# Rest tokens' loads behind the first pair's, four more operand slots at a change of blocks, and less on GpSimd, in a three-stage kernel on one core

## The chip, the cores and the metric

The kernel runs on one core of one Trainium2 chip. The metric is device time in microseconds (us) of one execution; lower is better. The times before come from three runs, and one further execution was recorded by the hardware profiler. TensorE (PE) does the matmuls, VectorE (DVE), ScalarE (ACT) and GpSimd (POOL) the element-wise work, and SyncE (SP) issues every data transfer.

## The reference

Three stages follow each other on 2304 tokens (4 batches of 576) of width 512.

```
q_s, k_s = q * scale, k * scale                       # 4 batches, 8 heads, seq 576, head_dim 64
phi(x): h = x @ omega.T - sum(x*x)/2;  exp(h - max(h)) / sqrt(128)
kv  = einsum('bhsm,bhsd->bhmd', phi(k_s), v);  z = sum of phi(k_s) over s
att = (phi(q_s) @ kv) / (phi(q_s) . z + 1e-6)
x   = att as 2304 x 512
y   = relu(x @ w_in)**2 @ w_out                       # first feed-forward, d_ff 2048
xn  = y / sqrt(mean(y*y) + 1e-6) * rms_g
out = (silu(xn @ w_gate) * (xn @ w_val)) @ w_out2     # second feed-forward, d_ff 1536
```

## The kernel before

**Tiles.** The tokens lie in five blocks: blocks 0 to 3 hold 512 tokens each (the first 512 of a batch), and the rest block holds the last 64 tokens of each batch, 256 in all. An fp32 operand is split into a high part (a cast on ACT, L403) and a low part (source minus high part, L394, on DVE or POOL); a product is then three fp32r matmul passes: high by high and the two mixed ones.

**Stages.** For each batch the attention goes over four pairs of heads; features of k and q are matmuls at L601, and k features times v at L671 (L674 for the rest tokens). A batch's rest tokens need three loads of their own, made by `rem_prep`: rest_t (the transposed tokens), rest_r (their rows, for the norms) and rest_v. The first feed-forward takes 16 chunks of 128 of its hidden width per block, at L845 (into PSUM bank h) and L875 (into acc), block by block between attention work; the rest block comes last, and L894 (DVE) and L890 (ACT) copy its results out of PSUM. Its output y goes to DRAM and is read back by the second feed-forward, which normalises it: `rms` finds the row factors, `scaled` loads a tile of y and multiplies it (L1020, DVE).

**The second feed-forward** runs on two groups of blocks: blocks 0 and 1, then blocks 2 and 3 with the rest block. In a group, a kind (gate or value) of a pair of chunks of 256 hidden columns by two blocks is made of seven products instead of eight (`seven`, L1081): they need sums and differences of the operands, called B11, T1, T2, T3, B22, B21 and T4. `operands` makes these per half (two halves kk of the width): four `scaled` loads, four subtractions (`minus`, L928), seven splits (`in_two`). The second half's loads wait for the last `minus` of the first (`gates`). The weights' sums are made beforehand and stored; `read_unit` loads them as tiles wq and splits them. `plus` (L1101, DVE) adds products up in tiles cc; `gated` makes silu (L1123, ACT) times value (L1126) and splits it into tiles ub (or g); `out_rows` multiplies those by the output weights (L1142) and adds into tiles oa (L1150, DVE).

**Order.** A planner (`Plan`) writes out the order of every engine's instructions ahead of time. Each piece of work has a priority (a due time), an engine or a choice of two ("ANY" in a split means DVE or POOL; `both_sbuf` and one branch of `gated` choose in the same way), and buffers that come from fixed numbers of slots by class: x 16, xa 12, xb 4, f 4, st 3, wq 8 and so on. Whatever the planner picked is what the engines execute, in order. `FILL` sets up to which planned time the planner puts matmuls of ones that compute nothing (L486, in pairs) where it sees TensorE without work. `lead` is the priority of the rest tokens' loads. SP issues all loads and stores in planned order.

Between the two groups, operands of the second group take slots: temporaries (`room`) from classes st and xb, the split operands from x and xa; xb also holds the loads of `rms`, and f its row factors.

Of the kernel before, what the change touches and what calls it, by code (L numbers as in the profile page):

```python
# [15 lines left out]
ALU = mybir.AluOpType  # L16
# [26 lines left out]
class Plan:  # L43
# [9 lines left out]


    COLD = 6.9
    FILL = (0.6, 65.0, 0.21)
    SPARE = {"DVE": 1.0, "ACT": 0.2, "POOL": 0.2}
    SPARE_TO = 200.0
    LAT = 0.27
# [45 lines left out]
    def fill(self):  # L105
        n = Node()
        n.eng, n.dur, n.tail, n.prio, n.idx = "PE", self.FILL[2], 0.0, 0.0, -1
        n.bufs, n.acq, n.outs, n.deps, n.alts = [], [], [], set(), []
# [139 lines left out]
def kernel(  # L248
# [23 lines left out]
    nc = tc.nc  # L272
# [35 lines left out]
    plan = Plan(slots)  # L308
# [60 lines left out]
    def f32(t):  # L369
        return t.bitcast(F32)  # L370
# [5 lines left out]
    def dve(n):  # L376
        return 0.07 + n * 0.00104

    def pool(n):
        return 0.19 + n * 0.00216  # L380
# [154 lines left out]
    def attention(b):  # L535
        base = (b - 1) * float(C1) if b else -25.0
        step = 3.7 if b else 6.0
        lead = base - (6.0 if b else 3.95)
        full, long = b < FULL, b >= LONG
        rem_x = []  # L540
        ssr = Buf(["sm"])
# [365 lines left out]
    NC2 = C2 // 2  # L907
# [4 lines left out]
    G0 = [E1, E1 + NC2 + 2.0]  # L912
# [10 lines left out]
            decode(pos, st, lambda: w.ap, w)  # L923
        return w

    def both_sbuf(prio, out, in0, in1, op, n, rd, wr):
        def tt(en):
            return lambda: en.tensor_tensor(out=out(), in0=in0(), in1=in1(), op=op)  # L928

        plan.add("DVE", Shared(dve(n)), prio, tt(nc.vector), rd, wr, alts=[("POOL", pool(n), tt(nc.gpsimd))])  # L930

    last = []

# [30 lines left out]
    def read_unit(c, nm, pos, gates):  # L964

        u = Buf(["wq"])
        dma(pos, lambda: f32(u.ap[:, 1, :]), lambda: w2_d[c, nm], 262144, r=[b_w2d[c, nm], b_w2a], w=[u], after=gates)
        split(pos, lambda: f32(u.ap[:, 1, :]), lambda: u.ap[:, 0, :], lambda: u.ap[:, 1, :], 512, [(u, 1)], (u, 0), (u, 1),
              "ANY")
        return u  # L970

    def read_units(c, pos, gates):
# [51 lines left out]
        return x  # L1024

    def minus(p0, out, a, b, n):
        both_sbuf(p0, lambda: out.ap[:, :n], lambda: a.ap[:, :n], lambda: b.ap[:, :n], ALU.subtract, n, [a, b], [out])

    def in_two(p0, x, cls, n):

        xh, xl = Buf(cls), Buf(cls)
        split(p0, lambda: x.ap[:, :n], lambda: xh.ap[:, :n], lambda: xl.ap[:, :n], n, [x], xh, xl, "ANY")
        return xh, xl

    def operands(j, rv, p0, cls, gates, room):
# [82 lines left out]
    def gated(prio, g, v, in_psum):  # L1118

        uh, ul = Buf(["ub", "g"]), Buf(["ub", "g"])  # L1120
        sb = Buf(["cc"]) if in_psum else g
        plan.add("ACT", act(512), prio,
                 lambda: nc.scalar.activation(out=sb.ap, in_=g.ap, func=AF.Silu), [g], [sb])  # L1123

        def mul(en):
            return lambda: en.tensor_tensor(out=sb.ap, in0=v.ap, in1=sb.ap, op=ALU.mult)  # L1126

        if in_psum:
            plan.add("DVE", dve(512), prio, mul(nc.vector), [v, sb], [sb])
        else:  # L1130
            plan.add("DVE", Shared(dve(512)), prio, mul(nc.vector), [v, sb], [sb], alts=[("POOL", pool(512), mul(nc.gpsimd))])
        split(prio, lambda: sb.ap, lambda: uh.ap, lambda: ul.ap, 512, [sb, b_w2b], uh, ul, "ANY")
        return uh, ul

# [97 lines left out]
    room = ["st", "dw"]  # L1232
# [4 lines left out]
    plan.add("NONE", 0.0, 0.0, open_w2b, w=[b_w2b], after=ph1_nodes)  # L1237
    sets = [read_units(c, E1 + (c - 1.0 if c else -7.0), []) for c in range(NC2)]
    hidden0 = moe2(0, sets, x01, None)
    room = ["st", "xb"]  # L1240
    rvr = rms(REM, G0[0] + 0.7, hidden0[:1], ["xb"], room, ["f"])
    xr2 = operands_rem(rvr, G0[0] + 2.0, hidden0[:1], room)
    rv23 = [rms(j, G0[0] + j - 0.3, hidden0[j - 1:j], ["xb"], room, ["f"]) for j in range(2, 4)]
    x23 = operands(2, rv23, G0[0] + NC2 - 0.5, ["x", "xa"], hidden0[3:4], room)
    sets = [read_units(c, G0[1] + c - 1.0, hidden0[4:5]) for c in range(NC2)]
    moe2(1, sets, x23, xr2)
    with tc.manual_schedule():
# [71 lines left out]
```

## Time and profile before

| what | value |
|---|---|
| runs (three) | 1003.1, 1006.02, 1006.41 us; median 1006.02 |
| profiled execution, its own time | 1006.28 us |
| its span (first to last instruction) | 1004.5 us |
| mean granted TensorE clock | 0.996 |
| PE busy | 989.2 us, 98% of the span |
| DVE, ACT, POOL busy | 712.2, 525.6, 122.3 us |
| DMA | 179.36 MB, mean 179 GB/s |

Busy time counts the time in which an engine had an instruction under way. The span is 1.8 us shorter than the execution's own time, and a change of the span is taken as a change of the time.

### The profile page before, as it was taken

The page shows a single profiled execution, that of the slowest core. Times are in us where ns is not written, and L with a number is a line of the kernel's source. Part 1 is how long each engine was busy: PE and PEld are TensorE (multiplying, and loading weights), DVE is VectorE, ACT ScalarE, POOL GpSimd, SP SyncE. Part 2 cuts the span into 40 slices and gives each one's busy share as a digit, 9 for nine tenths or more (in the row PEclk, how much of TensorE's full clock was granted, in tenths as well). Part 3 has the DMA queues.
Part 4 walks back from the last instruction along what each step waited for, and adds up shares of the span by engine and source line. Part 5 has one row for each costly group of instructions (what it writes and reads, how often), then busy time and mean ns, then how long its engine had stood idle before and what let it go on. Part 6 is the DMA issues. An engine that isn't in the chain of part 4 may idle for free.

```text
span 1004.5 us, 14617 instructions
## 1 busy us (share of the span) xinstructions
PE 989.2 (98%) x5140; PEld 838.4 (83%) x5140; DVE 712.2 (71%) x1374; ACT 525.6 (52%) x1097; POOL 122.3 (12%) x101
## 2 busy tenths in 40 slices
PE   8999999999999999999999999999998999999998
PEld 7888888888888888888789978888886888888887
DVE  5989998577658576655622879889797747576673
ACT  5878888545564555544534557654353444224220
POOL 0110132131110101100000302311043000000000
PEclk9999999999999999999999999999999999999999
DMA  7777888976667575678868435234243212212213
GB/s 244 255 243 251 280 263 307 303 256 228 242 216 260 188 247 185 226 255 286 281 216 267 146 106 162 80 116 137 75 123 108 83 53 63 74 31 79 71 32 104
DMA packets 74841, 179.36 MB, mean 179 GB/s; under 512 B 8848, under 2 KB 12048, under 8 KB 74768
## 3 DMA queue, kind: packets, MB, share of 16 engines
q1 hardware_dynamic: 74768, 178.43, 54.2%
q8 instruction: 40, 0.66, 0.3%
q14 instruction: 33, 0.27, 0.1%
HBM read 143.27 MB, written 35.13 MB: 178 GB/s over the span
## 4 chain that ended last, share of the span: by engine, by line
PE 88%; DVE 4%; DMA 4%; issue 1%; ACT 1%; POOL 1%; SPq 0%; ACTq 0%; POOLq 0%; DVEq 0%
PE acc L875 18%; PE h L845 18%; PE acc L1081 11%; PE t L1142 11%; PE h L1081 10%; PE t L1081 3%; PE t L731 3%; PE t L604 2%; PE t L601 2%; PE t L671 2%; DMA st<-y 2%; PE t L726 1%; PE h L1142 1%; DVE cc L1101 1%; DVE wq L394 1%
## 5 line engine op out<-in xcount | busy, mean ns | idle before, releaser
L875 PE MATMUL acc<-g,wr 128*128 128x512 f32 (+1 forms) x660 | 151.7, 374 | 0.7 <-DVE g L394 0.7
L845 PE MATMUL h<-x,wr 128*128 128x512 f32 x528 | 133.4, 396 | 0.0
L875 PEld LDWEIGHTS acc<-g,wr 128*128 128x128 f32 x660 | 113.6, 189 | 21.3 <-DVE g L394 1.5
L1142 PE MATMUL t<-wq,ub 128*128 128x512 f32 x462 | 114.5, 392 | 0.7 <-DVE oa L1150 0.7
L1081 PE MATMUL acc<-x,wq 128*128 128x512 f32 x321 | 111.5, 396 | 1.8 <-DVE f L894 1.8
L845 PEld LDWEIGHTS h<-x,wr 128*128 128x128 f32 x528 | 97.2, 188 | 19.2
L403 ACT CAST wq<-wq 128x512 fp32r<-128x512 f32 x108 | 66.3, 619 | 87.3 <-DMA wq<-w2d4g 14.8
L1142 PEld LDWEIGHTS t<-wq,ub 128*128 128x128 f32 x462 | 86.7, 189 | 20.6 <-DVE oa L1150 2.4
L394 DVE TENSOR_TENSOR g<-f,g 128x512 fp32r<-128x512 f32 (+1 forms) x67 | 46.4, 693 | 70.1 <-ACT f L515 58.8
L859 ACT ACTIVATE f<-h 128x512 f32<-128x512 f32 (+1 forms) x80 | 44.9, 562 | 92.4 <-PE h L845 86.1
L1081 PE MATMUL acc<-xa,wq 128*128 128x512 f32 x231 | 89.9, 396 | 3.1 <-ACT xa L403 3.1
L394 DVE TENSOR_TENSOR wq<-wq 128x512 fp32r<-128x512 f32 x99 | 74.1, 756 | 25.5 <-ACT wq L403 25.0
L1081 PE MATMUL h<-x,wq 128*128 128x512 f32 x255 | 81.0, 390 | 0.0
L1081 PEld LDWEIGHTS acc<-x,wq 128*128 128x128 f32 x321 | 61.1, 191 | 15.1 <-DVE f L894 2.3
L875 PE MATMUL acc<-g,wu 128*128 128x512 f32 (+1 forms) x300 | 70.7, 376 | 0.2 <-DVE g L394 0.2
L1081 PE MATMUL h<-xa,wq 128*128 128x512 f32 x201 | 69.3, 390 | 0.4 <-DVE xa L394 0.4
L628 ACT ACTIVATE p<-t,sm 128x128 f32<-128x128 f32 x216 | 60.0, 383 | 18.1 <-DVE sm L619 18.1
L1101 DVE TENSOR_TENSOR cc<-acc,cc 128x512 f32<-128x512 f32 x84 | 57.7, 686 | 14.8 <-PE acc L1081 13.8
L1150 DVE TENSOR_TENSOR oa<-t,oa 128x512 f32<-128x512 f32 x75 | 50.8, 686 | 23.1 <-PE t L1142 22.7
L845 PE MATMUL h<-x,wu 128*128 128x512 f32 x240 | 61.6, 398 | 0.0
L875 PEld LDWEIGHTS acc<-g,wu 128*128 128x128 f32 x300 | 51.5, 189 | 9.5 <-DVE g L394 0.8
L441 ACT ACTIVATE dw<-st 128x512 f32<-128x512 f32 x68 | 46.6, 696 | 22.8 <-DMA st<-in_w_out_dram 9.4
(245 smaller groups left out, 1818.8 us busy)
## 6 DMA issues: line engine op xcount, KB each, us to landing
wr<-w1d SPq DMA_DIRECT2D x88, 512.0 KB, 4.3
st<-in_w_out_dram SPq DMA_DIRECT2D x28, 512.0 KB, 4.7
w1d<-wr SPq DMA_DIRECT2D x22, 512.0 KB, 4.1
st<-in_w_in_dram SPq DMA_DIRECT2D x16, 512.0 KB, 4.5
st<-in_w_gate_dram SPq DMA_DIRECT2D x12, 512.0 KB, 5.9
st<-in_w_val_dram SPq DMA_DIRECT2D x12, 512.0 KB, 5.9
st<-y SPq DMA_DIRECT2D x23, 256.0 KB, 4.1
v<-in_v_r_dram SPq DMA_DIRECT2D x16, 260.0 KB, 3.2
```

What stands on the lines that cost most here:

```text
L394: return lambda: en.tensor_tensor(out=lo(), in0=src(), in1=f32(hi()), op=ALU.subtract)
L403: first = plan.add("ACT", act(n), prio, lambda: nc.scalar.copy(out=hi(), in_=src()), rd, [whi], after, pre=[blo] if blo is not bhi else [])
L441: lambda: nc.scalar.activation(out=out(), in_=hf(), func=AF.Abs, scale=65536.0), [(st, 1)], [w])
L628: nc.scalar.activation(out=pbuf.ap[:, j0 + i, :], in_=fp.ap[:, i, :], func=AF.Exp, bias=mx.ap[:, i:i + 1])
L731: nc.tensor.matmul(np.ap[:, r * D1:(r + 1) * D1], lhsT=qt.ap[:, r * P:(r + 1) * P], rhs=kvt[:, h, :], start=True, stop=True)
L845: nc.tensor.matmul(hb.ap[:, :n], lhsT=u.ap[:, wl, kk * P:(kk + 1) * P], rhs=xcols(j, xl, kk)(), start=(gi == 0 and ii == 0), stop=(gi == l ...
L859: lambda: nc.scalar.activation(out=rb.ap[:, :n], in_=hb.ap[:, :n], func=AF.Relu), [hb], [rb])
L875: nc.tensor.matmul(accs[e].ap[:, :n], lhsT=u.ap[:, w, es], rhs=x.ap[:, :n], start=(c == 0 and i == 0), stop=(c == C1 - 1 and i == 2))
L1081: nc.tensor.matmul(bank.ap[:, cols], lhsT=u.ap[:, wl, c0 + kk * P:c0 + (kk + 1) * P], rhs=x[kk][xl].ap[:, :cols.stop - cols.start], start= ...
L1101: lambda: nc.vector.tensor_tensor(out=out.ap, in0=bank.ap, in1=x.ap, op=ALU.add), [bank, x], [out])
L1142: nc.tensor.matmul(o.ap, lhsT=x[xl].ap[:, c0:c0 + P], rhs=us[f"o{i}"].ap[:, wl, :], start=i == n == 0, stop=i == 1 and n == 2)
L1150: lambda: nc.vector.tensor_tensor(out=oa.ap, in0=o.ap, in1=oa.ap, op=ALU.add), [o, oa], [oa])
```

## The change

```
--- before.py
+++ after.py
@@ -53,7 +53,7 @@
 
 
     COLD = 6.9
-    FILL = (0.6, 65.0, 0.21)
+    FILL = (0.6, 45.0, 0.21)
     SPARE = {"DVE": 1.0, "ACT": 0.2, "POOL": 0.2}
     SPARE_TO = 200.0
     LAT = 0.27
@@ -535,7 +535,7 @@
     def attention(b):
         base = (b - 1) * float(C1) if b else -25.0
         step = 3.7 if b else 6.0
-        lead = base - (6.0 if b else 3.95)
+        lead = base - (6.0 if b else 2.85)
         full, long = b < FULL, b >= LONG
         rem_x = []
         ssr = Buf(["sm"])
@@ -923,11 +923,12 @@
             decode(pos, st, lambda: w.ap, w)
         return w
 
-    def both_sbuf(prio, out, in0, in1, op, n, rd, wr):
+    def both_sbuf(prio, out, in0, in1, op, n, rd, wr, pool_too=True):
         def tt(en):
             return lambda: en.tensor_tensor(out=out(), in0=in0(), in1=in1(), op=op)
 
-        plan.add("DVE", Shared(dve(n)), prio, tt(nc.vector), rd, wr, alts=[("POOL", pool(n), tt(nc.gpsimd))])
+        plan.add("DVE", Shared(dve(n)), prio, tt(nc.vector), rd, wr,
+                 alts=[("POOL", pool(n), tt(nc.gpsimd))] if pool_too else [])
 
     last = []
 
@@ -966,7 +967,7 @@
         u = Buf(["wq"])
         dma(pos, lambda: f32(u.ap[:, 1, :]), lambda: w2_d[c, nm], 262144, r=[b_w2d[c, nm], b_w2a], w=[u], after=gates)
         split(pos, lambda: f32(u.ap[:, 1, :]), lambda: u.ap[:, 0, :], lambda: u.ap[:, 1, :], 512, [(u, 1)], (u, 0), (u, 1),
-              "ANY")
+              "DVE")
         return u
 
     def read_units(c, pos, gates):
@@ -1024,12 +1025,12 @@
         return x
 
     def minus(p0, out, a, b, n):
-        both_sbuf(p0, lambda: out.ap[:, :n], lambda: a.ap[:, :n], lambda: b.ap[:, :n], ALU.subtract, n, [a, b], [out])
+        both_sbuf(p0, lambda: out.ap[:, :n], lambda: a.ap[:, :n], lambda: b.ap[:, :n], ALU.subtract, n, [a, b], [out], False)
 
     def in_two(p0, x, cls, n):
 
         xh, xl = Buf(cls), Buf(cls)
-        split(p0, lambda: x.ap[:, :n], lambda: xh.ap[:, :n], lambda: xl.ap[:, :n], n, [x], xh, xl, "ANY")
+        split(p0, lambda: x.ap[:, :n], lambda: xh.ap[:, :n], lambda: xl.ap[:, :n], n, [x], xh, xl, "DVE")
         return xh, xl
 
     def operands(j, rv, p0, cls, gates, room):
@@ -1128,7 +1129,7 @@
         if in_psum:
             plan.add("DVE", dve(512), prio, mul(nc.vector), [v, sb], [sb])
         else:
-            plan.add("DVE", Shared(dve(512)), prio, mul(nc.vector), [v, sb], [sb], alts=[("POOL", pool(512), mul(nc.gpsimd))])
+            plan.add("DVE", Shared(dve(512)), prio, mul(nc.vector), [v, sb], [sb])
         split(prio, lambda: sb.ap, lambda: uh.ap, lambda: ul.ap, 512, [sb, b_w2b], uh, ul, "ANY")
         return uh, ul
 
@@ -1237,11 +1238,11 @@
     plan.add("NONE", 0.0, 0.0, open_w2b, w=[b_w2b], after=ph1_nodes)
     sets = [read_units(c, E1 + (c - 1.0 if c else -7.0), []) for c in range(NC2)]
     hidden0 = moe2(0, sets, x01, None)
-    room = ["st", "xb"]
+    room = ["st", "f"]
     rvr = rms(REM, G0[0] + 0.7, hidden0[:1], ["xb"], room, ["f"])
     xr2 = operands_rem(rvr, G0[0] + 2.0, hidden0[:1], room)
     rv23 = [rms(j, G0[0] + j - 0.3, hidden0[j - 1:j], ["xb"], room, ["f"]) for j in range(2, 4)]
-    x23 = operands(2, rv23, G0[0] + NC2 - 0.5, ["x", "xa"], hidden0[3:4], room)
+    x23 = operands(2, rv23, G0[0] + NC2 - 0.5, ["x", "xa", "xb"], hidden0[3:4], room)
     sets = [read_units(c, G0[1] + c - 1.0, hidden0[4:5]) for c in range(NC2)]
     moe2(1, sets, x23, xr2)
     with tc.manual_schedule():
```

The whole of it, in words. Fillers are planned up to 45 us of planned time instead of 65. The rest loads of batch 0 get a later priority. In the second feed-forward, the low part of the split weights and of the operands, the subtractions of `minus` and the product in `gated` can now go to DVE only; the split behind that product may still go to POOL. For the second group, temporaries come from st and f instead of st and xb, and the split operands may also take the four xb slots. From L931 on line numbers are one higher (L1082 is L1081 of before, L1151 is L1150, and so on).

By count, over the whole program: POOL has 18 fewer instructions of L394, one fewer of L928 and of L1126, and five more of L514 (squares for the attention's row norms). DVE has 18 more of L394, one more of L928 and L1126 each, two more of L437 and three fewer at L516 and L510. ACT has four fewer of L515, two fewer of L435 and two more of L509. PE has ten fewer matmul records of L486. SP has as many transfers as before.

**SP at the start of the program.** Names ahead of `<-` are buffers with their numbers; `in_k_t_dram` and so on are inputs. Before:

```order
L388 DMA om_76<-in_omega_t_dram 64x128 x2
L388 DMA lt_190<-in_rest_t_dram 128x512
L388 DMA ld_195<-in_rest_r_dram 128x512
L388 DMA vr<-in_rest_v_dram 64x520
L388 DMA lt_206<-in_k_t_dram 128x512
L388 DMA tt_215<-in_q_t_dram 128x512
L388 DMA ld_221<-in_k_r_dram 128x512
L388 DMA ld_229<-in_q_r_dram 128x512
L388 DMA v_82<-in_v_r_dram 128x520
```

With the change:

```order
L388 DMA om_76<-in_omega_t_dram 64x128 x2
L388 DMA lt_190<-in_k_t_dram 128x512
L388 DMA lt_195<-in_q_t_dram 128x512
L388 DMA ld_202<-in_k_r_dram 128x512
L388 DMA ld_211<-in_q_r_dram 128x512
L388 DMA v_82<-in_v_r_dram 128x520
L388 DMA tr_222<-in_rest_t_dram 128x512
L388 DMA ld_228<-in_rest_r_dram 128x512
L388 DMA vr<-in_rest_v_dram 64x520
```

The first pair's five loads (k and q in two layouts, v) moved ahead of the three rest loads; the eight together hold the same places as before.

**DVE where the first feed-forward ends and the second begins.** Buffers dw and st hold loaded and subtracted operands, x and xa their low parts, g low parts of the first feed-forward's rest block. Before:

```order
L928 TENSOR_TENSOR dw_6175<-dw_5607,dw_6175 128x512
L394 TENSOR_TENSOR x_6260<-st_5630,x_6259 128x512
L394 TENSOR_TENSOR x_6289<-dw_6175,x_6288 128x512
L928 TENSOR_TENSOR dw_6175<-st_5630,dw_6175 128x512
L516 TENSOR_TENSOR f_6306<-f_6306 128x256
L394 TENSOR_TENSOR g_6317<-f_6306,g_6316 128x256
L394 TENSOR_TENSOR x_6327<-dw_6175,x_6326 128x512
L1020 SCALAR_TENSOR_TENSOR st_6324<-wq_5279,g_sb,st_6324 128x512
L1020 SCALAR_TENSOR_TENSOR st_6334<-wq_5426,g_sb,st_6334 128x512
```

With the change:

```order
L928 TENSOR_TENSOR dw_6164<-dw_5597,dw_6164 128x512
L394 TENSOR_TENSOR x_6209<-st_5550,x_6208 128x512
L394 TENSOR_TENSOR x_6231<-dw_6164,x_6230 128x512
L1021 SCALAR_TENSOR_TENSOR st_5620<-wq_5269,g_sb,st_5620 128x512
L394 TENSOR_TENSOR g_6245<-f_6238,g_6244 128x256
L928 TENSOR_TENSOR dw_6164<-st_5620,dw_6164 128x512
L394 TENSOR_TENSOR x_6268<-st_5620,x_6267 128x512
L394 TENSOR_TENSOR x_6283<-dw_6164,x_6282 128x512
L394 TENSOR_TENSOR g_6289<-f_6274,g_6288 128x256
L1021 SCALAR_TENSOR_TENSOR st_6280<-wq_5269,g_sb,st_6280 128x512
L1021 SCALAR_TENSOR_TENSOR st_6295<-wq_5416,g_sb,st_6295 128x512
```

The last `minus` of the first half, on which the second half's loads wait, is `dw_6175<-st_5630` before and `dw_6164<-st_5620` with the change. It stood behind the low parts x_6260 (of B21) and x_6289 (of the difference T2); now B21's low part (x_6268) stands behind it, T2's (x_6231) is three rows ahead, and a g of the first feed-forward stands right ahead. The low parts of x that POOL made before are among DVE's rows now.

**ACT at the same place**: L859 takes the relu of the first feed-forward's h out of PSUM, so it waits for TensorE; L403 casts the second feed-forward's operands. Before:

```order
L403 CAST x_6259<-st_5630 128x512
L859 ACTIVATE f_6282<-h_6244 128x256
L403 CAST x_6288<-dw_6175 128x512
L861 ACTIVATE g_6295<-f_6282 128x256
L515 ACTIVATE f_6282<-f_6282 128x256
```

With the change:

```order
L403 CAST x_6230<-dw_6164 128x512
L859 ACTIVATE f_6238<-h_6191 128x256
L861 ACTIVATE g_6244<-f_6238 128x256
L515 ACTIVATE f_6238<-f_6238 128x256
L403 CAST x_6267<-st_5620 128x512
```

T2's cast (x_6288, now x_6230) stood behind an L859 and now stands ahead of the one that follows.

**PE where the second group of blocks takes over.** t and h at L1142 are results of `out_rows` of the first group; L1081 with x, xa or xb are products of the second group. Before:

```order
L1081 MATMUL acc_7992<-x_7735,wq_7945 128x512
L1081 MATMUL acc_7992<-x_7960,wq_7945 128x512
L1081 MATMUL acc_7993<-x_7795,wq_7949 128x512
L1081 MATMUL acc_7993<-xa_8012,wq_7949 128x512
L1081 MATMUL acc_7993<-x_7796,wq_7949 128x512
L1081 MATMUL acc_7993<-xa_8013,wq_7949 128x512
L1081 MATMUL acc_7993<-x_7795,wq_7949 128x512
L1081 MATMUL acc_7993<-xa_8012,wq_7949 128x512
L1142 MATMUL t_8030<-wq_7718,ub_7906 128x512 x2
L1142 MATMUL t_8030<-wq_7718,ub_7907 128x512
L1142 MATMUL t_8030<-wq_7756,ub_7867 128x512 x2
L1142 MATMUL t_8030<-wq_7756,ub_7868 128x512
```

With the change:

```order
L1143 MATMUL h_8018<-wq_7717,ub_7880 128x512 x2
L1143 MATMUL h_8018<-wq_7717,ub_7881 128x512
L1143 MATMUL h_8018<-wq_7755,ub_7852 128x512 x2
L1143 MATMUL h_8018<-wq_7755,ub_7853 128x512
L1143 MATMUL t_8029<-wq_7717,ub_7880 128x512 x2
L1143 MATMUL t_8029<-wq_7717,ub_7881 128x512
L1143 MATMUL t_8029<-wq_7755,ub_7852 128x512 x2
L1143 MATMUL t_8029<-wq_7755,ub_7853 128x512
L1082 MATMUL h_8041<-xb_7451,wq_7796 128x512
L1082 MATMUL h_8041<-x_7911,wq_7796 128x512
L1082 MATMUL h_8041<-xb_7452,wq_7796 128x512
L1082 MATMUL h_8041<-x_7912,wq_7796 128x512
```

Before, two products of the second group (12 rows, of which seven are shown) stood ahead of the last four row products of the first group; now all row products of the first group stand ahead of the second group's first product, whose operands are xb and x.

**DVE in the middle of the first group** has rows that make two of the second group's operands early, in slots of class xb. With the change:

```order
L1021 SCALAR_TENSOR_TENSOR st_7373<-f_6783,g_sb,st_7373 128x512
L1021 SCALAR_TENSOR_TENSOR st_7383<-f_7115,g_sb,st_7383 128x512
L1102 TENSOR_TENSOR cc_7440<-acc_7418,cc_7439 128x512
L928 TENSOR_TENSOR f_7456<-st_7383,st_7373 128x512
L394 TENSOR_TENSOR wq_7426<-wq_7426 128x512
L394 TENSOR_TENSOR wq_7430<-wq_7430 128x512
L394 TENSOR_TENSOR xb_7452<-st_7373,xb_7451 128x512
L1102 TENSOR_TENSOR cc_7441<-acc_7418,cc_7439 128x512
```

Before, no xb slot was open to these operands. Here the two L1021 rows, the `minus` into `f_7456` and the low part `xb_7452` belong to the second group; the rows of wq and cc among them belong to the first.

## Rows read from the trace of the kernel before

**Rows 1.** Profile page: the chain that ended last, share of the span by engine.
```profile
PE 88%; DVE 4%; DMA 4%; issue 1%; ACT 1%; POOL 1%; SPq 0%; ACTq 0%; POOLq 0%; DVEq 0%
```

**Rows 2.** Waits of PE: line, releaser; us in total, times, longest.
```profile
PE acc L1081 <- ACT xa L403: 3.1, 1, 3.1
PE acc L1081 <- DVE f L894: 1.8, 1, 1.8
...
PE h L1081 <- DVE xa L394: 0.4, 1, 0.4
```

**Rows 3.** Windows: length, PE, PEld, DVE, ACT, POOL busy (instructions), PE clock, DMA, GB/s.
```profile
584.00:588.00 4.00, 4.00 (x13) 3.12 (x12) 1.46 (x4) 2.63 (x4) 0.00 (x0) 0.57 0.23 70
762.00:766.00 4.00, 4.00 (x12) 2.69 (x12) 4.00 (x7) 1.24 (x2) 1.28 (x1) 0.63 0.17 66
```

**Rows 4.** Timeline from the start: begin, duration, engine, line; what ended the wait.
```profile
5.05 2.04 PE L601 MATMUL t<-bd,lt 128*128 128x256 f32 x4 [1.07 <-DMA lt<-in_rest_t_dram]
...
5.67 0.43 SPq L388 DMA_DIRECT2D v<-in_v_r_dram  x1
...
8.77 2.07 PE L601 MATMUL h<-bd,lt 128*128 128x256 f32 x4 [1.25 <-DMA lt<-in_k_t_dram]
...
17.08 1.00 PE L671 MATMUL h<-v,p 128*128 128x65 f32 x8
```

**Rows 5.** Windows of longer stretches, columns as in Rows 3.
```profile
25.00:125.00 100.00, 100.00 (x576) 85.28 (x576) 93.35 (x243) 83.34 (x202) 13.27 (x10) 1.00 0.77 259
600.00:765.00 165.00, 161.88 (x705) 132.69 (x704) 144.86 (x208) 87.57 (x152) 38.14 (x28) 0.99 0.37 109
743.00:765.00 22.00, 18.88 (x75) 14.55 (x74) 20.38 (x26) 7.72 (x14) 12.99 (x9) 0.92 0.20 66
```

**Rows 6.** Timeline, the last fillers.
```profile
58.77 1.78 PE L486 MATMUL acc<-ones 128*128 128x256 f32 x12
58.93 0.68 DVE L394 TENSOR_TENSOR x<-acc,x 128x512 fp32r<-128x512 f32 x1
```

**Rows 7.** Timeline, where the second feed-forward begins.
```profile
557.84 0.97 POOL L394 TENSOR_TENSOR g<-f,g 128x256 fp32r<-128x256 f32 x1 [2.81 <-ACT f L515]
...
567.32 0.38 ACT L859 ACTIVATE f<-h 128x256 f32<-128x256 f32 x1 [1.42 <-PE h L845]
...
568.97 0.69 DVE L928 TENSOR_TENSOR dw<-st,dw 128x512 f32<-128x512 f32 x1
...
572.24 1.41 DVE L1020 SCALAR_TENSOR_TENSOR st<-wq,g_sb,st 128x512 f32<-128x512 f32 x2
...
574.33 0.60 ACT L403 CAST x<-st 128x512 fp32r<-128x512 f32 x1
...
574.51 0.43 DVE L394 TENSOR_TENSOR g<-f,g 128x256 fp32r<-128x256 f32 x1 [0.87 <-issue]
...
574.99 1.57 PE L875 MATMUL acc<-g,wr 128*128 128x256 f32 x11 [0.39 <-DVE g L394]
...
582.80 0.75 DVE L894 COPY f<-acc 128x256 f32<-128x256 f32 x2
583.27 2.75 PE L1081 MATMUL acc<-x,wq 128*128 128x512 f32 x7 [1.84 <-DVE f L894]
```

**Rows 8.** Timeline, where the second group begins.
```profile
756.18 1.78 DVE L928 TENSOR_TENSOR st<-st,st 128x512 f32<-128x512 f32 x1
757.37 1.72 POOL L394 TENSOR_TENSOR x<-xb,x 128x512 fp32r<-128x512 f32 x1
...
761.56 0.79 PE L1081 MATMUL acc<-xa,wq 128*128 128x512 f32 x1 [3.12 <-ACT xa L403]
```

**Rows 9.** Groups by shape, 590 to 765: busy us, mean ns; idle before and releaser.
```profile
L1150 DVE TENSOR_TENSOR oa<-t,oa 128x512 f32<-128x512 f32 x26 | 17.5, 683 | 3.4 <-PE t L1142 3.4
L1126 DVE TENSOR_TENSOR cc<-cc,cc 128x512 f32<-128x512 f32 x17 | 13.5, 816 | 0.1
L394 DVE TENSOR_TENSOR ub<-cc,ub 128x512 fp32r<-128x512 f32 x15 | 12.6, 839 | 1.4 <-ACT ub L403 1.3
```

## Prediction: what the change should do to the time

> **What bounds the kernel now.** I read four views, in this order. The chain that ended last is 88% TensorE's [rows 1], and PE is busy for nearly the whole span, so a change pays only where PE idles or runs at a low clock. The waits of PE say where it idles: most of it is at two changes of stage, 3.1 us for operands of the second group and 1.8 us for a PSUM copy where the second feed-forward begins, with 0.4 us more at the latter [rows 2]. The windows add what the waits don't show: behind each of these idle stretches the granted clock falls. It is 0.57 over 584 to 588 and 0.63 over 762 to 766, which at full PE busy loses 4 x 0.43 = 1.7 us and 4 x 0.37 = 1.5 us [rows 3]. Third comes the start: PE waits 1.07 and 1.25 us for first loads, and the first real sum, k features times v, stands at 17.08 [rows 4]. Between these places PE is fully busy and no engine can win anything there.
>
> **The change, part by part.** The sum is made against the profiled execution, 1006.28 us, 0.26 above the median of the three runs, which is less than I can tell.
>
> *Rest loads behind the first pair's.* The load at the head of SP's queue is there at 5.05; the k load, which stood fourth, is there at 8.77 [rows 4]. So k's features can begin up to 8.77 - 5.05 = 3.7 us earlier. The product with v, however, also needs k's rows, v and, on PE and ACT, a turn among the rest tokens' work. The eight loads together hold the same places, so the last of them, issued at 5.67, does not come sooner. And what follows is not waiting for PE alone: from 25 to 125 DVE is busy 93% and ACT 83% [rows 5], so part of a head start is eaten there. Bounds 0 and 3.7; I take 1.2, a third.
>
> *No fillers behind 45 us of planned time.* Ten matmul records of PE go, in essence the twelve at 58.77. They hold PE until about 60.4 (58.77 + 1.6), whereas the low part that the next product awaits is ready at 58.93 + 0.68 = 59.61 [rows 6]. So 0.8 of the 1.6 us is gained, and the other 0.8 becomes a wait for DVE. Bounds 0 and 0.8, unless the clock falls (below). Together: 2.0.
>
> *Where the second feed-forward begins.* The last `minus` of the first half starts at 568.97, and only then are the second half's four loads issued, whose first L1020 follows at 572.24 [rows 7]. What made that `minus` late: ACT's cast of T2 stood behind an L859 that waited 1.42 us for TensorE [rows 7], and in the changed order that cast stands ahead of the L859. Also, DVE instructions beside POOL are stretched: an L928 that overlaps a POOL L394 takes 1.78 where DVE's undisturbed tiles of that size take 0.68, so 1.1 more [rows 8, 9], and the POOL splits of x are gone here. That is 1.42 + 1.1 = 2.5 us, more than the 1.84 that PE waits behind L894 [rows 7], whose DVE work is the tail of the same chain. So the 1.84 and the 0.42 go, and the clock's 1.7 in part, as it fell behind these. Against it: the last g low part, behind which PE waits 0.39, goes to POOL (0.97 for such a tile against DVE's 0.43, so +0.54), and a cast of 0.60 now stands ahead of its input on ACT [rows 7]. That wait becomes 0.39 + 0.54 + 0.60 = 1.5, and with it some of the clock's loss stays, 0.7 by my choice (less than half, as the idle stretch is shorter than the 2.65 of before). Gain: 0.39 + 0.42 + 1.84 + 1.7 - 1.5 - 0.7 = 2.1. Bounds: -1.1 (only the new 1.1 us of wait arrives) and 4.3 (all of it goes).
>
> *Where the second group begins.* Before, PE met the second group's products while DVE and ACT were still making operands, 3.12 idle at 761.56 [rows 8] and 1.5 at the low clock. Now two things come together. B11 and T2 of the first half are made early, into xb slots that were closed to them. And the first group's last four row products stand ahead: 161.88 us busy for 705 records is 0.23 each, 1.38 for the six of a product [rows 5], so 4 x 1.38 = 5.5 us more cover. Not all is covered: behind the last sum of the first group DVE has 34 instructions up to the first weight's low part. Each takes 0.68 [rows 9], about 0.62 from start to start, 21 us; PE's cover is 15 row products, 20.7 us. The waits for a PSUM bank and for ACT in that chain are worth some more, so I leave 1.0 us of idle or slow clock: 4.6 - 1.0 = 3.6. Bounds: 1.0 (DVE's chain as late as before, less the earlier two operands) and 4.6.
>
> *Off GpSimd.* Of POOL's 28 instructions from 600 to 765 [rows 5], 24 go to DVE: 19 of 512 columns at 0.683 and five of 256 at about 0.42, 15.1 us. DVE is idle there 165 - 144.86 = 20.1 us, so they fit, and the sharing gives some back: L1126 17 x (816 - 683) ns = 2.3 and the ub splits 15 x (839 - 683) ns = 2.3, 4.6 us in these two groups alone [rows 9]. Cost on PE: none while DVE runs ahead of it. In the last 22 us DVE idles only 1.6 [rows 5], but there POOL's nine become some 5.5 us of DVE against 13 us of overlap; this is in the 34 instructions above.
>
> The Trainium skill ("SBUF — State Buffer", section "SBUF: two separate sides") says that VectorE and GpSimd take one port pair as an exclusive lock, the other blocking for the whole instruction. The 1.78 against 0.68 agrees. By that rule alone the 24 instructions would give back as much DVE time as they took on POOL, by an estimate some 33 us (38.14 less the four that stay), and DVE would end up far lighter. The rows show only 4.6 in the two groups where it is plainest. By either DVE stays off the path of 600 to 743, so the sum is the same.
>
> **Sum:** 1006.28 - 2.0 - 2.1 - 3.6 = 998.6.
>
> **Rivals.**
>
> *The start's head start is hidden.* The first products need the rest tokens' loads or DVE and ACT anyway; then 1.2 of the first 2.0 goes, and a shortfall of 0.7 in the same crowded stretch is likely: 1000.5. For it: DVE's 93%. Against: PE plainly waits for k.
>
> *The clock falls where fillers were.* PE idles 0.8 us at 58.77 and runs below full clock after it, as it did behind both other idle stretches [rows 3]: the 0.8 gained becomes a loss of about 0.8, and if the wait of 1.5 keeps the whole 1.7 at 584 the term there is 1.1. 1006.28 - 0.4 - 1.1 - 3.6 = 1001.2. Against it: only longer idle shows a fall in these rows. The Trainium skill ("TensorE: Matmul & The Clock Gate", section "🔬 Part 1: The HAM clock gate (the "warmup" mystery)") speaks against the edit: the throttled state is the default there, and activity releases it. By that the twelve fillers had a use.
>
> *DVE's chains are not earlier.* What came off POOL fills the room that the changes of stage had: the terms there shrink to 0 and 1.0 and the start's to 1.2, 1004.1, hardly to be told from before. For it: DVE is full in the last 22 us. Against: the stretched rows become short.
>
> *DVE becomes the bound* in the first group, so slower: it takes 15.1 us more with nothing given back, in bursts that PSUM banks and cc tiles can't bridge. It decides from about 7.5 us (half) that PE sees, with the last term lost: 1006.28 - 2.0 - 2.1 + 7.5 = 1009.7. For it: ready casts wait behind what is queued on DVE. Against: 20 us of idle, and shorter rows.
>
> **How the numbers follow.** My forecast gets 0.52, and its own range is 996 to 1001; the hidden start 0.15, the clock 0.12, the late chains 0.13, slower 0.08. The time is the likeliest, 998.6. All terms at their best give 1006.28 - 3.7 - 0.8 - 4.3 - 4.6 = 992.9, which needs all at once, so the range begins at 994. It ends at 1004, in the case of the late chains, and leaves out that case's upper half, the slower one and the tails. A measurement of this kernel can't tell less than 0.3%, 3 us, from no change: below 1003.0 counts as faster, which holds the first three cases but for a tail, 0.78. The same: 0.14, mostly the late chains. Above 1009.0: 0.08.
>
> **What would show it.** Right: L671 begins near 15 to 16; no wait behind L894; the wait for g at the end of the first feed-forward 1 to 2 us; the wait at the second group's first product under 1 us and the clock of 0.63 gone; POOL's busy time some 33 us lower over 600 to 765 with DVE at over 150 of 165 and PE still busy. Wrong: L671 still at 17; a clock below 1.00 around 60; DVE without idle in 600 to 743 while PE shows waits on L1102, L1127 or ub; a new wait on xb or f, as the row factors and the temporaries now share four f slots.

## The result, and the profile after

The changed kernel takes 996.78 us (median of four runs, 995.74 to 997.85) against 1006.21 us of before (four runs, 1003.1 to 1007.34): ratio 0.9914, 95% interval 0.9893 to 0.9935. The forecast was 998.6 in a range of 994 to 1004. The profiled execution has a span of 994.4 us, 10.1 less.

First the waits of PE, columns as in [rows 2]:

```profile
PE t L601 <- ACT p L628: 1.9, 2, 1.7
PE t L1143 <- DVE oa L1151: 1.4, 5, 0.7
PE acc L875 <- DVE g L394: 1.4, 3, 1.0
PE t L601 <- DMA lt<-in_k_t_dram: 1.2, 1, 1.2
PE acc L875 <- POOL g L394: 1.2, 1, 1.2
```

The three rows of [rows 2] are gone, and what is left is small pieces. Three that matter below are new: 1.7 us for `p`, where fillers stood, 1.2 us for a g on POOL, and the 0.7 among those for row results (oa). The windows, columns as in [rows 3]:

```profile
576.00:588.00 12.00, 12.00 (x55) 9.93 (x54) 9.35 (x17) 7.19 (x13) 0.00 (x0) 1.00 0.45 122
594.00:755.00 161.00, 160.17 (x705) 131.58 (x704) 145.21 (x231) 87.18 (x151) 5.17 (x4) 1.00 0.37 113
590.00:745.00 155.00, 154.92 (x684) 127.85 (x683) 138.22 (x219) 85.09 (x148) 5.17 (x4) 1.00 0.38 112
752.00:756.00 4.00, 3.92 (x18) 2.90 (x17) 4.00 (x7) 0.50 (x1) 0.00 (x0) 1.00 0.58 216
```

The clock no longer falls where the second feed-forward begins, nor where the groups change (last row). The second row holds as many matmul records, 705, as the second of [rows 5], in 161 us instead of 165. DVE has 231 instructions there instead of 208 and is busy for 145.21 us instead of 144.86, while POOL fell from 38.14 to 5.17.

And the timeline, at the places of [rows 4, 6 to 8]:

```profile
5.20 3.46 PE L601 MATMUL t<-bd,lt 128*128 128x256 f32 x8 [1.22 <-DMA lt<-in_k_t_dram]
...
15.09 1.00 PE L671 MATMUL h<-v,p 128*128 128x65 f32 x8
...
58.31 0.70 PE L601 MATMUL t<-bd,lt 128*128 128x256 f32 x2 [1.72 <-ACT p L628]
...
563.83 0.68 DVE L928 TENSOR_TENSOR dw<-st,dw 128x512 f32<-128x512 f32 x1
...
571.43 0.60 ACT L403 CAST xa<-dw 128x512 fp32r<-128x512 f32 x1
...
572.43 0.91 POOL L394 TENSOR_TENSOR g<-f,g 128x256 fp32r<-128x256 f32 x1 [2.51 <-ACT f L515]
...
573.39 1.57 PE L875 MATMUL acc<-g,wr 128*128 128x256 f32 x11 [1.18 <-POOL g L394]
...
578.69 0.74 DVE L894 COPY f<-acc 128x256 f32<-128x256 f32 x2
578.91 1.75 PE L1082 MATMUL acc<-x,wq 128*128 128x512 f32 x7
...
751.39 3.36 PE L1143 MATMUL t<-wq,ub 128*128 128x512 f32 x12 [0.67 <-DVE oa L1151]
```

Rows that answer to each other give the gain by stage. The eleven matmuls that wait for g are at 573.39 instead of 574.99, so 1.6 us were won up to there. This is 2.4 us won ahead of the g wait, less the wait's growth by 0.8 (0.39 to 1.18). The seven matmuls behind L894 are at 578.91 instead of 583.27: 4.36, of which 2.76 were won between the two. The clock of 0.57 that followed there [rows 3] is 1.00 now, 1.7 more. That makes 1.6 + 2.76 + 1.7 = 6.1; the rest of the 10.1, 4.0 us, was won behind that, at the change of groups. These are two single executions. How far the first of these numbers can be trusted is asked below, under only_loads.

### The profile page after: what moved, and what is told of

Its sections match the earlier page's. It is cut to its first block, busy times and chain, and to the rows that moved or that the text cites. A ratio compares the mean times of both kernels' runs of the same rounds, so it can differ in the third digit from the quotient of the medians.

```text
span 994.4 us, 14580 instructions
## 1 busy us (share of the span) xinstructions
PE 980.4 (99%) x5130; PEld 832.7 (84%) x5130; DVE 712.0 (72%) x1393; ACT 523.7 (53%) x1093; POOL 100.5 (10%) x86
## 4 chain that ended last, share of the span: by engine, by line
PE 86%; DVE 7%; DMA 3%; issue 1%; ACT 1%; SPq 0%; POOL 0%; ACTq 0%; DVEq 0%; POOLq 0%
PE acc L875 18%; PE h L845 18%; PE acc L1082 11%; PE t L1143 10%; PE h L1082 10%; PE t L1082 3%; PE t L731 3%; PE t L604 3%; PE t L671 2%; PE t L601 2%; DMA st<-y 2%; PE t L726 1%; DVE cc L1102 1%; PE h L1143 1%; DVE oa L1151 1%
## 5 line engine op out<-in xcount | busy, mean ns | idle before, releaser
L1143 PE MATMUL t<-wq,ub 128*128 128x512 f32 x474 | 116.8, 391 | 1.5 <-DVE oa L1151 1.4
L403 ACT CAST wq<-wq 128x512 fp32r<-128x512 f32 x108 | 66.3, 619 | 98.1 <-DMA wq<-w2d3g 17.7
L1082 PE MATMUL acc<-x,wq 128*128 128x512 f32 x324 | 106.9, 389 | 0.0
L394 DVE TENSOR_TENSOR wq<-wq 128x512 fp32r<-128x512 f32 x108 | 77.5, 726 | 29.5 <-ACT wq L403 29.2
L394 DVE TENSOR_TENSOR g<-f,g 128x512 fp32r<-128x512 f32 (+1 forms) x68 | 49.6, 729 | 65.9 <-ACT f L515 55.4
L859 ACT ACTIVATE f<-h 128x512 f32<-128x512 f32 (+1 forms) x80 | 45.1, 564 | 90.0 <-PE h L845 87.2
L1082 PE MATMUL h<-x,wq 128*128 128x512 f32 x252 | 85.3, 390 | 0.0
L1082 PEld LDWEIGHTS acc<-x,wq 128*128 128x128 f32 x324 | 60.8, 188 | 12.7
L1082 PE MATMUL acc<-xa,wq 128*128 128x512 f32 x192 | 69.8, 389 | 0.0
L1151 DVE TENSOR_TENSOR oa<-t,oa 128x512 f32<-128x512 f32 x75 | 50.9, 687 | 21.8 <-PE t L1143 21.3
L1082 PE MATMUL h<-xa,wq 128*128 128x512 f32 x168 | 60.5, 389 | 0.0
```

The costliest lines, as they stand in the source:

```text
L394: return lambda: en.tensor_tensor(out=lo(), in0=src(), in1=f32(hi()), op=ALU.subtract)
L403: first = plan.add("ACT", act(n), prio, lambda: nc.scalar.copy(out=hi(), in_=src()), rd, [whi], after, pre=[blo] if blo is not bhi else [])
L859: lambda: nc.scalar.activation(out=rb.ap[:, :n], in_=hb.ap[:, :n], func=AF.Relu), [hb], [rb])
L1082: nc.tensor.matmul(bank.ap[:, cols], lhsT=u.ap[:, wl, c0 + kk * P:c0 + (kk + 1) * P], rhs=x[kk][xl].ap[:, :cols.stop - cols.start], start= ...
L1143: nc.tensor.matmul(o.ap, lhsT=x[xl].ap[:, c0:c0 + P], rhs=us[f"o{i}"].ap[:, wl, :], start=i == n == 0, stop=i == 1 and n == 2)
L1151: lambda: nc.vector.tensor_tensor(out=oa.ap, in0=o.ap, in1=oa.ap, op=ALU.add), [o, oa], [oa])
```

## The experiments

The kernels ran in three sets of four, each set on one chip together with the kernel before: only_loads, only_dve, only_slots and no_slots (before: median 1004.36 us, 27 runs); no_dve, full_again, no_fill and ns_adds_3 (1004.13, 17 runs); full_adds_3, ub_twice, last_g_dve and full_adds_g (1004.16, 25 runs). Ratios are to the kernel before of the same set, with a 95% interval; they differ a little from the quotient of the two medians. Kernels of different sets are compared by their ratios.

### Each part by itself, and all but one

**only_loads.**

```
-        lead = base - (6.0 if b else 3.95)
+        lead = base - (6.0 if b else 2.85)
```

> Only the later priority of the rest loads; fillers still planned up to 65 us (and more of them than before, 48 records of L486 in the order instead of 26), POOL and slots as before. My theory: the start alone is worth about 2 us (the first product with v began at 15.09 instead of 17.08 in the changed kernel) and both changes of stage stay as they were, so about 1004 us against 1006.2 of before, L671 at 15.1, the waits of 3.1 and 1.8 us and the two low clocks still there. Rival (the head start is hidden, DVE and ACT eat it by 125 us): 1006, no difference. Second rival (the start is the larger part of the 9.4 us): 1001 or less.

1005.32 us, 1.0012 (1.0000 to 1.0024): no gain. This is not the loads alone, since the trace has 50 filler matmuls (L486) here instead of 26. L671 began at 14.32, but three more runs show what that is worth. Each line is the first L671 of a kernel: only_dve and only_slots, whose start is that of before, and then no_slots, with the new order of loads.

```profile
14.90 1.00 PE L671 MATMUL h<-v,p 128*128 128x65 f32 x8
...
14.61 1.00 PE L671 MATMUL h<-v,p 128*128 128x65 f32 x8
...
16.64 1.00 PE L671 MATMUL h<-v,p 128*128 128x65 f32 x8
```

The old order gives 14.6 to 17.1 (three executions), the new one 14.2 to 16.6 (eleven). The start differs by 2 us from execution to execution, more than the order moves it.

For the larger part this is TensorE's clock. In the profiled execution of before, four matmuls of one size took 1.85 us just ahead of 14 us and 1.03 just behind (first two rows). In no_slots the granted clock was 0.50 over 11 to 14, which is 1.2 of 2.4 GHz (third row, a window); its wait for the rest load had ended at 10.31, nearly as in the changed kernel (10.22), and still its L671 came 1.55 us later:

```profile
12.34 1.85 PE L601 MATMUL t<-bd,tt 128*128 128x256 f32 x4
14.03 1.03 PE L601 MATMUL h<-bd,tt 128*128 128x256 f32 x4
...
11.00:14.00 3.00, 3.00 (x10) 2.44 (x9) 2.15 (x9) 2.86 (x11) 0.27 (x1) 0.50 0.93 311
```

Before, no_slots and no_fill are the three executions with L671 at 16.5 or later; in the other eleven no such slow matmuls are left behind 11 us. So the 2.4 us that were won ahead of the g wait can be in good part the luck of two executions: up to that wait the three executions with the old loads took 571.4 to 574.6 us, and the nine with the new loads and the shorter fillers took 569.6 to 574.2.

**only_dve.** The edits of the diff in `both_sbuf`, `read_unit`, `minus`, `in_two` and `gated`, for instance:

```
-        split(p0, ..., n, [x], xh, xl, "ANY")
+        split(p0, ..., n, [x], xh, xl, "DVE")
```

> Only the work off GpSimd; loads, fillers and slots as before. The order of TensorE at the change of groups shows all row products of the first group ahead of the second group's first product already here. My theory: the second feed-forward's beginning gains its 3.7 us and the change of groups most of its 4.1, say 3, so 999.5 us; no wait behind L894, clock 1.00 over 576 to 590, a wait of 0 to 1.5 us at the second group's first products. Rival (the slots bring the gain at the change of groups): only 3.7 us, 1002.5, with 3 us of wait at the change of groups. Second rival (DVE becomes the bound without the start's slack): 1006 or more.

1001.40 us, 0.9974 (0.9960 to 0.9987): nearer to the first rival's size than to my theory's. The beginning of the second feed-forward is as in the changed kernel (L894 at 577.85, TensorE behind it at 578.07 without a wait). At the change of groups the first group's row products do stand ahead, and still TensorE waits, now for a bank of their own results; all rows are from only_dve, with a window over the wait and one that goes on behind it:

```profile
752.40 1.27 DVE L1151 TENSOR_TENSOR oa<-t,oa 128x512 f32<-128x512 f32 x2
...
753.23 2.97 PE L1143 MATMUL t<-wq,ub 128*128 128x512 f32 x12 [3.45 <-ACT xa L403]
...
749.78:753.23 3.45, 0.00 (x1) 0.03 (x1) 3.45 (x7) 1.24 (x2) 0.00 (x0) 1.00 0.00 0
752.00:760.00 8.00, 6.77 (x30) 5.66 (x31) 7.84 (x14) 0.62 (x1) 0.00 (x0) 1.00 0.61 213
```

The releaser named is ACT's xa, but the row product needs a bank of t that DVE's additions empty, and those stand behind a run of second-group operands on DVE, which is busy throughout the wait (3.45 of 3.45 us). This is read from the order and the times; ns_adds_3 below tests it.

**only_slots.**

```
-    room = ["st", "xb"]
+    room = ["st", "f"]
-    x23 = operands(..., ["x", "xa"], hidden0[3:4], room)
+    x23 = operands(..., ["x", "xa", "xb"], hidden0[3:4], room)
```

> Only the classes of slots: temporaries from st and f, operands also in xb; POOL, loads and fillers as before. In the order of TensorE one product of the second group, instead of two, stands ahead of the first group's last four row products. My theory: early operands help little without DVE's order: about 1 us, 1005, the wait at the change of groups still 2 to 3 us with the clock low behind it, the wait of 1.8 us behind L894 unchanged. Rival (the slots are what matters there): that wait under 1 us, clock 1.00, 4 us won, 1002.

1005.16 us, 1.0016 (0.9997 to 1.0034): nothing. TensorE now waits three times at the change of groups instead of once: 1.2 us for an addition of row results on DVE, 0.9 for a copy by ACT (cc), and 2.2 for an operand's low part.

**no_slots**: all but that edit.

> All of the change but the classes of slots. My theory: within 1 us of the changed kernel, about 997.5, with 14 row products of the first group ahead of the second group's first product and a wait of at most 1.5 us there. Rival (the slots are needed for the last term): 4 us lost against the changed kernel, 1001, with a wait of 3 us and the clock down to 0.5 to 0.6 behind it.

999.08 us, 0.9950 (0.9933 to 0.9967), 3.9 us short of the whole change (0.9911 in full_again): the rival. The wait is that of only_dve to a hundredth; but the clock behind it is another:

```profile
754.24 4.57 PE L1143 MATMUL t<-wq,ub 128*128 128x512 f32 x12 [3.45 <-ACT xa L403]
...
753.00:761.00 8.00, 6.76 (x23) 5.44 (x24) 6.32 (x11) 0.62 (x1) 0.00 (x0) 0.79 0.53 193
```

The same instructions with the same idle time ran on at 1.00 in one execution and at a mean of 0.79 in the other, 8 x 0.21 = 1.7 us.

**no_dve**: all but the edits of only_dve.

> All of the change but the work off GpSimd, which POOL may take again. Theory A (what leaves GpSimd is the whole of the gain at the beginning of the second feed-forward, and slots alone lose at the change of groups): the waits of 0.4 and 1.8 us and the low clock near 580 are back, the wait at the change of groups is 2 us or more; 1002.5 us or a ratio of 0.997 to 1.001. Theory B (loads, fillers and slots carry half of the gain by themselves): ratio 0.995 or less.

1002.47 us, 0.9984 (0.9968 to 0.9999), as theory A had it. Waits like the old ones are back, 1.8 us behind L894 and 2.2 us for a second-group operand instead of 3.1:

```profile
PE acc L1081 <- DVE xa L394: 2.2, 1, 2.2
PE acc L1081 <- DVE f L894: 1.8, 1, 1.8
```

**full_again**: the changed kernel beside these. **no_fill**: the changed kernel with

```
-    FILL = (0.6, 45.0, 0.21)
+    FILL = (0.6, 65.0, 0.21)
```

> The changed kernel itself once more, so that it stands on one chip and in the same rounds as the kernels beside it. If the first result was typical: ratio 0.989 to 0.994. If part of it was the luck of four runs (the start and the clock differ from execution to execution): 0.994 to 0.997.

> All of the change but the end of the fillers, which are planned up to 65 us again: 48 filler records of L486 instead of 16, the rest of TensorE's order at both changes of stage as in the changed kernel. Theory A (the fillers hold TensorE longer than the waits that they fill): 32 records at 0.134 us are 4.3 us, against waits of 1.7 and 0.4 us near 55 to 60 us in the changed kernel that they would cover, so about 2 us slower than the changed kernel. Theory B (they only fill waits): the same time. Theory C (they hold the clock up): faster than the changed kernel, whose granted clock would have to be below 1.00 between 50 and 100 us.

The changed kernel: 995.43 us, 0.9911 (0.9892 to 0.9931). With fillers up to 65: 996.61 us, 0.9921 (0.9903 to 0.9938). The two can't be told apart, and theory A's 2 us lie within the same noise, so A and B both stay open. Theory C finds no support in the times. The windows of both, 54 to 58, the changed kernel first:

```profile
54.00:58.00 4.00, 3.66 (x11) 2.55 (x12) 2.56 (x10) 1.35 (x3) 0.00 (x0) 0.65 0.77 263
...
54.00:58.00 4.00, 4.00 (x28) 3.47 (x28) 2.54 (x10) 1.61 (x4) 0.00 (x0) 1.00 0.59 197
```

In this execution of the changed kernel the clock did fall, to a mean of 0.65 in the window. In that of the first result it stayed at 1.00. The fall stands behind two shorter waits and ahead of the new one for `p`:

```profile
52.79 1.11 PE L731 MATMUL t<-kv,qt 128*128 128x65 f32 x8 [0.74 <-ACT qt L509]
54.34 1.27 PE L601 MATMUL t<-bd,lt 128*128 128x256 f32 x4 [0.45 <-DVE xw L707]
...
60.48 0.70 PE L601 MATMUL t<-bd,lt 128*128 128x256 f32 x2 [1.72 <-ACT p L628]
```

All nine executions with the shorter fillers have this wait of 1.72 us, and behind it the clock stayed at 1.00 in each. The fillers' edit without the loads' was not run.

### What the change of groups waits for

**ns_adds_3**: no_slots, with the additions of row results ahead on DVE.

```
-            plan.add("DVE", dve(512), prio,
+            plan.add("DVE", dve(512), prio - 3.0,
                      lambda: nc.vector.tensor_tensor(out=oa.ap, in0=o.ap, in1=oa.ap, op=ALU.add), [o, oa], [oa])
```

> All of the change but the classes of slots, and the additions of row results (L1150) get a priority 3 steps earlier, so that on DVE they stand among the second group's operands instead of behind a run of fifteen of them. Theory A (the 3.5 us that TensorE waits without the slots is DVE's order: row results lie in PSUM behind a run of operand work): that wait is under 1 us, nothing like it comes back at the second group's first product beyond 1.5 us, and the ratio is 0.993 or less. Theory B (DVE has simply too much work between the groups, wherever it stands): the wait moves to the second group's products with 3 us or more, ratio 0.995 as without it.

996.63 us, 0.9915 (0.9896 to 0.9935): theory A. Another order of DVE's queue gives back 3.5 of the 3.9 us that the slots were worth; the intervals of the two kernels just touch, but the stall is gone. TensorE goes through the row products, and later it waits 1.8 us for a weight's low part that DVE makes last, 0.3 more than theory A allowed. The profiled execution is the slowest of the six, with a granted clock of 0.66 over 760 to 765, behind that wait.

**full_adds_3**: the same edit on the changed kernel.

> The changed kernel, with the additions of row results 3 steps earlier in priority. Theory A (the 0.7 us for a row result at the change of groups is the rest of the same stall in DVE's order): that wait is gone, nothing takes its place, ratio 0.990. Theory B (DVE is full there, so the weights' low parts come later instead, as in the run without the slots, where TensorE waited 1.8 us for one): a wait of 1 to 2 us for wq in its place, ratio 0.991 to 0.993. In the second group the four waits of 0.17 us for these additions should go in either case.

997.14 us, 0.9920 (0.9902 to 0.9938): theory B. The 0.67 is gone and this has come:

```profile
757.92 0.50 PE L1082 MATMUL h<-xb,wq 128*128 128x512 f32 x1 [1.73 <-DVE wq L394]
```

The four waits in the second group are gone, too, as expected, and in the first group there is a new one of 0.74 us for a row result, at 707.

**ub_twice.**

```
-        split(prio, lambda: sb.ap, lambda: uh.ap, lambda: ul.ap, 512, [sb, b_w2b], uh, ul, "ANY")
+        split(prio, lambda: sb.ap, lambda: uh.ap, lambda: ul.ap, 512, [sb, b_w2b], uh, ul, "DVE")
+        less(prio, lambda: sb.ap, lambda: uh.ap, lambda: ul.ap, 512, [sb, uh, b_w2b], [ul], "DVE")
```

> The changed kernel, with the low part of every gated tile made on DVE (POOL's last ones in the second feed-forward go) and made twice, the second time into the same tile with the same result. In the first group that is some 22 more DVE instructions and four from POOL, 26 x 0.683 = 17.8 us, against 16.8 us that DVE idles from 590 to 752 in the changed kernel. Theory A (DVE stood just short of being the bound in the first group; the change had used 15 of its 20 us): TensorE now waits for DVE there, 2 to 6 us slower than the changed kernel, ratio 0.993 to 0.997. Theory B (PSUM banks and tiles decouple them so far that only the changes of stage matter): no wait of PE between 600 and 735, ratio 0.990 to 0.992. Rival C (DVE was the bound already): 17 us slower, ratio above 1.005.

999.18 us, 0.9944 (0.9925 to 0.9963), 3.3 us slower than the changed kernel: theory A's size, but at theory B's place. The window, and the wait:

```profile
590.00:745.00 155.00, 154.64 (x674) 125.59 (x674) 148.07 (x242) 83.34 (x143) 0.00 (x0) 1.00 0.37 111
...
PE t L1144 <- ACT xa L403: 2.5, 1, 2.5
...
752.76 0.68 DVE L1152 TENSOR_TENSOR oa<-t,oa 128x512 f32<-128x512 f32 x1
```

With DVE busy for 148 of 155 us TensorE still misses only 0.4 us inside the group. The price falls due at its end, as in only_dve: a row product waits from 751.14 to 753.59, and the addition that empties its bank runs at 752.76, behind a run of second-group operands on DVE.

### The wait for POOL's g

**last_g_dve.**

```
-            less(base + c, ..., [rb, gh], [gl], "ANY")
+            less(base + c, ..., [rb, gh], [gl],
+                 "DVE" if j == REM and c >= C1 - 2 else "ANY")
```

> The changed kernel, with the low parts g of the rest block's last two chunks on DVE only. Theory A (the 1.2 us that TensorE waits for POOL's last g is the price of that one POOL instruction and the cast ahead of its input): the wait is 0.4 to 0.7 us, 0.6 us won, which is about what can be told; the ratio 0.990 to 0.991 if the change of groups stays as it is. The planner, however, sets two products of the second group ahead of 14 row products there, instead of one ahead of 15; theory B (such a shift brings a wait back, as without the slots): 1 to 3 us of wait at the change of groups, ratio 0.991 to 0.993.

1003.30 us, 0.9993 (0.9976 to 1.0010): neither theory; 8 us of the gain are lost by moving two instructions and by the order that the planner then makes. On DVE's timeline the last g comes behind all but one of the low parts of the second feed-forward's second half, and TensorE with it:

```profile
576.51 0.42 DVE L394 TENSOR_TENSOR g<-f,g 128x256 fp32r<-128x256 f32 x1
...
576.99 2.08 PE L876 MATMUL acc<-g,wr 128*128 128x256 f32 x8 [5.84 <-DVE g L394]
```

Behind this wait the granted clock was 0.50 over 577 to 581, and at the change of groups 1.6 us of wait for a row result came, as theory B had it.

**full_adds_g**: the additions' edit, and the last chunk's g alone on DVE.

> Both: the additions 3 steps earlier and the low part g of the rest block's last chunk on DVE only. If both small waits are what they seem and the planner's order holds: 0.6 and 0.7 us less wait, ratio 0.9895 to 0.9905. If each takes its room from other work on DVE: as the changed kernel, 0.991 to 0.992.

1003.85 us, 0.9990 (0.9977 to 1.0003), with a wait of 6.4 us for the same g. No version tried beats the changed kernel.

## Why the prediction was right, step by step

*What bounds the kernel.* Right: all that was won lies at idle or slow stretches of TensorE, and between them nothing moved. The granted clocks of the runs beside each other give an estimate of the clock's part: a mean of 0.9954 for 17 runs of before, 0.9992 for six of the changed kernel, so about 0.0038 x 1004 = 3.8 us of the 8.7 won there.

*Rest loads and fillers, 2.0.* Not shown, though the profiled pair gives 2.4. The first L671 came at 15.09, inside the 15 to 16 that I named, but with the loads as before it came at 14.61 and 14.90 as well, so that sign came true by luck. The 17.08 that I started from goes with a slow clock, which no_slots and no_fill have with the new order, too. By themselves the loads win nothing (1.0012, with 24 more fillers), and the fillers' edit can't be told from none (0.9911 against 0.9921). Two pairs speak for the two edits together: no_slots is 2.3 us faster than only_dve, and no_dve has 0.9984 where only_slots has 1.0016, 3.2 us. In each pair the intervals overlap, and the rival of a hidden start stays open. The step "0.8 of the 1.6 us is gained" was wrong in its working: what TensorE would wait for was not the low part at 59.61 but ACT's `p`, behind a changed order, and those 1.72 us are as long as the 1.6 us of fillers. The rival of the clock had a mechanism (0.65 in one execution, behind waits of 0.74 and 0.45 us), but no price of it shows: the kernel with the longer fillers has the higher median, by 1.2 us.

*The second feed-forward's beginning, 2.1.* Mechanism right, size too small. The gate, the last `minus`, is 5.1 us earlier; 2.4 of this is the earlier start, and the other 2.7 are near the 2.5 that I worked out. L894 is 4.1 earlier, and PE no longer waits behind it. A `minus` ahead of the gate shows what I had called stretched, before and after:

```profile
564.56 1.78 DVE L928 TENSOR_TENSOR dw<-dw,dw 128x512 f32<-128x512 f32 x1
...
560.46 0.68 DVE L928 TENSOR_TENSOR dw<-dw,dw 128x512 f32<-128x512 f32 x1
```

The new wait for g is 1.18, where I had 1.5, of the composition named: a cast ahead and POOL's 0.91. The sum is 2.76 + 1.7 - 0.8 = 3.7. The term that was mis-sized most is the clock: of the 1.7 I left 0.7, and nothing stayed. Beside it, the g wait took 0.3 less, and the two waits that went were worth 2.76 instead of their 2.26. It came in only_dve as well and went in no_dve, so it is shown to be GpSimd's part of the change. The 1.7 is not in every execution, though: only_slots has the same waits there as before, and its clock stayed at 1.00 over 576 to 590.

*The change of groups, 3.6.* Right in size (4.0), and in that 0.67 of wait stayed where I had left 1.0. Wrong was the weight of its two causes. I gave the row products that stand ahead "5.5 us more cover"; in only_dve and no_slots they stand ahead and cover little, because each needs a bank that DVE empties, and DVE was in the middle of the operands. Slots alone win nothing either. What wins is that fewer operand instructions stand ahead of the additions on DVE: ns_adds_3 gets 3.5 us from DVE's order alone. So the two edits must be read together: off GpSimd is worth 1004.36 - 1001.40 = 3.0 us without slots, loads and fillers, and 1002.47 - 995.43 = 7.0 us with them. The rival of the late chains, that the terms at the two changes of stage shrink to 0 and 1.0, is refuted by the 3.7 and the 4.0.

*Off GpSimd at no cost.* Right, and by more than the 4.6 us that I counted as given back. The 23 more DVE instructions in as many matmuls cost 145.21 - 144.86 = 0.35 us of busy time. Of the 15.1 us that I had for what moves, some 14.7 came back, so the sign "DVE at over 150 of 165" did not come. In the two groups that I had counted, ub's low parts fell from 839 ns [rows 9] to 684, as I had it, and L1126 from 816 only to 764. More came from the operands' own instructions, which I had not counted; for instance (before, 590 to 765; after, 580 to 752):

```profile
L928 DVE TENSOR_TENSOR st<-st,st 128x512 f32<-128x512 f32 x2 | 2.5, 1230 | 0.0
...
L928 DVE TENSOR_TENSOR st<-st,st 128x512 f32<-128x512 f32 x2 | 1.4, 681 | 0.0
L394 DVE TENSOR_TENSOR ub<-cc,ub 128x512 fp32r<-128x512 f32 x18 | 12.2, 684 | 1.1 <-ACT ub L403 1.1
```

The Trainium skill ("SBUF — State Buffer", section "SBUF: two separate sides") has VectorE and GpSimd block each other for a whole instruction. This agrees in kind; the 33 us that the prediction estimated by it are more than twice what came back. Rival "DVE becomes the bound" is refuted: even ub_twice, with 10 us more of DVE, leaves TensorE busy inside the group.

## What to carry to other kernels

Take small work off GpSimd where it runs beside a full VectorE: here VectorE did it for next to nothing, since its own instructions became shorter. But ask of each instruction what will stand ahead of it in the new queue: moving two short ones to VectorE cost 8 us, because a run of the next stage's operands was queued first. Where a product waits at a change of stage, look past the named releaser to whoever empties its PSUM bank. And before a start or a clock is read from one profile, look at how far it differs between executions.

## What the runs showed of the hardware

Two kernels with the same 3.45 us of idle TensorE, to the hundredth, went on at a granted clock of 1.00 and of 0.79. The same two waits at the beginning of the second feed-forward, 0.42 and 1.84 us, were followed by 0.57 over 4 us in before and by 1.00 in only_slots. And behind the same wait of 1.72 us, which ends between 57 and 61, the clock stayed at 1.00 in nine executions out of nine. Idle time is therefore worth more than its length on the mean; a fall cost some 1.7 us in before and in no_slots. The Trainium skill ("TensorE: Matmul & The Clock Gate", section "🔬 Part 1: The HAM clock gate (the "warmup" mystery)") says that activity releases a throttle that is there by default; the falls behind idle stretches agree with it. Why one such stretch is followed by a fall and another is not, no run here shows.

The first loads land at times that differ, too: TensorE's wait for the first k load ended at 8.77, 7.61 and 7.98 in the three executions with the old order. The clock of the first 14 us adds to this, and the first L671 comes up to 2.5 us apart in executions of one order (14.61 and 17.08).
